# Own leading columns for each key slot, another split of the first tile's chunk sums, and new instruction orders in a one-core attention and gated-MLP kernel

## The chip, the cores and the metric

The kernel runs on one core of a Trainium2 chip. The core has five engines, each with its own instruction queue: TensorE (PE, with weight loads shown apart as PEld), VectorE (DVE), ScalarE (ACT), GpSimd (POOL) and SyncE (SP), which here only issues DMA transfers. ScalarE issues some transfers as well. Engines meet through semaphores. The metric is the device time of one execution in microseconds; smaller is better.

## The reference

The input x has 2048 tokens of 512 values. It is normalised, and the sum of two branches is added to it.

```
def _A_ref(x, wqkv, wo):                 # x is the normalised input
    H = 32; Dh = 16; W, dil = (8, 2)
    q, k, v = x @ wqkv                   # per head
    idx = pos[:, None] - off[None, :]    # each token sees itself and 7 tokens, 2 apart, behind it
    logits = einsum('bhsd,bhswd->bhsw', q, kg) * scale      # kg = k at idx; masked where idx < 0
    attn = softmax(logits)
    return einsum('bhsw,bhswd->bhsd', attn, vg) @ wo

def _B_ref(x, w_in, w_sp, b_sp, w_out):
    z = gelu(x @ w_in); z1 = z[..., :Fh]; z2 = layernorm(z[..., Fh:])     # Fh = 896
    g = einsum('ts,bsf->btf', w_sp, z2) + b_sp[None, :, None]             # 2048 x 2048 mix over tokens
    return (z1 * g) @ w_out

return x + _A_ref(xn, A_wqkv, A_wo) + _B_ref(xn, B_w_in, B_w_sp, B_b_sp, B_w_out)
```

## The kernel before

All on-chip data lie in one bf16 arena. Work is written as named tasks; a planner (`Plan`) works out dependences from the ranges that each task reads and writes, and puts in the semaphore waits. The order of the tasks on each engine is written out by hand in `plan.orders`: five lists, for TensorE, ScalarE, VectorE, GpSimd and SyncE's queue. An engine never passes a task that waits. The tasks that matter here are these, b being a block of 128 tokens, j a tile of four blocks (512 tokens), c one of four chunks of 128 of the 512 q and k columns, and t one of eight pairs of output blocks:

- `ldx b` loads a block of x; `bnst b`, `bnag b` (VectorE, L647, L650), `rstd b` (GpSimd, a power, L652) and `norm b` (VectorE, L662) normalise it; `xTd b` (SyncE, L666) transposes it by DMA. Blocks 0 to 3 are transposed on TensorE (`xTr`, `xTe`).
- `ldq` and `ldk` (L602) load the q and the k half of the attention weights.
- `Q j_c` and `K j_c` (TensorE, L730) are four matmuls each; `QKe j_c` (ScalarE, L738) evicts both from PSUM to a slot of q and of k, slot j mod 2.
- `prod j_c` (VectorE, L754) multiplies q by the eight shifted copies of k. It reads up to 14 columns ahead of the tile's own. For odd j these are the end of slot 0, which lies directly ahead of slot 1; for even j they are 16 leading columns (`KTpad`) ahead of slot 0, zero for tile 0 (`ktpad`) and copied by ScalarE from the end of slot 1 for tile 2 (`halo c`, L744).
- `padd j_n` (VectorE, L759) adds chunk products together; `lg j_0` (TensorE, L769) sums over the rows of a head with 8 matmuls for each array of products it is given, in tiles of 32 columns. In tile 0 chunks 0 to 2 are added on VectorE and the array of chunk 3 goes to TensorE by itself (`npadd` (1, 2)), so lg0_0 has 16 matmuls; in the other tiles all four are added first and there are 8. `lge j` (ScalarE, L791) evicts the logits.
- `z2_b`, `z1_b` (TensorE, L849, L892) and `V b` (L714) are the other projections, `z2g`, `z1g`, `Ve` their evictions on ScalarE, `z2s` (L904) squares for the variance. `zm, zq, ze, zv, zb j` are small VectorE steps of the second normalisation, `zr j` (L923) its power on GpSimd, `zn b` applies it (L930 on ScalarE for tiles 0 and 1, L934 on VectorE for 2 and 3). `T1` to `T4 j` (L951) are differences and sums of halves of z2.
- `pT`, `sm`, `ssub`, `sexp`, `sz`, `srec`, `sattn` are the softmax, by transposed tiles of logits.
- For each pair t: `w t` loads and transposes rows of w_sp (L959), `S13, S2, S4 t` (VectorE) add them, seven products `P1` to `P7` (TensorE, L1012) mix the tokens, `cA, cE, cB, g11, g21` (ScalarE) and `g12, g22` (VectorE) finish the gate, `u b` multiplies by z1 and `uT b` transposes the result; `pv b`, `pva`, `pvc t` (VectorE, L1142 to L1150) weigh the values and `OTd t` (L1154) transposes the attention output; `out b` (TensorE, L1204 and L1208) forms 512 output columns from `OTd` and `uT`, on top of x (`os`), and `fin` evicts them; `st` stores.
- `hm0` to `hm2` (GpSimd) make the head selector of lg, `mask0`, `mask1` the mask tile `maskt` that `smask` adds to tile 0; `ldb` loads b_sp into `bsb` and `biasf` (ScalarE) converts it. `Vhaloa`, `Vhalob`, `Vzero` shift v by a token row for pv.

Of PSUM's eight banks lg holds 6 and 7 and the projections share 0 to 5 in pairs, so a group waits for the eviction of the group three ahead of it.

Of the kernel before, what the change touches and what calls it, by code (L numbers as in the profile page):

```python
# [325 lines left out]
def build_kernel(nc, A_x, A_wqkv, A_wo, B_x, B_w_in, B_w_sp, B_b_sp, B_w_out, out, report=False, sched_kw=None,  # L326
# [88 lines left out]
    with ExitStack() as es:  # L415
# [808 lines left out]
        for t in range(NT):  # L1224
# [11 lines left out]
            if t >= 1:  # L1236
# [23 lines left out]
                z1g7 z1g5 zn5 z1g4 z1g2 z2s15 zn0 z1g0 z1g3 z1g1 lge3 Ve12 zn1 Ve13 zn2 Ve15 Ve14 zn3 Ve10 Ve7 Ve11  # L1260
                Ve6 ldxr1 Ve8 Ve9 ldxr0 Ve4 sexp3 Ve5 Ve2 Ve0 cA_0 Ve1 cE_0 Ve3 cB_0 sexp2 biasf g11_0 cA_1 g21_0 cE_1
                os12_0 cB_1 g11_1 os14_0 sexp1 g21_1 cA_2 cE_2 os15_0 cB_2 g11_2 cA_3 cB_3 g21_2 ldxr2 g11_3 fin14_0
                fin15_0 os13_0 cE_3 cA_4 st0_0_0 cB_4 g21_3 g11_4 fin12_0 os10_0 ldxr3 cE_4 fin13_0 os11_0 st1_0_0
                ldxr4 sexp0 cA_5 g21_4 os8_0 fin11_0 os6_0 cB_5 fin10_0 g11_5 cE_5 cE_6 cA_6 os9_0 g11_6 fin8_0
# [85 lines left out]
```

## Time and profile before

| | |
|---|---|
| time, median of 3 runs | 229.22 us (229.14 to 229.64) |
| profiled execution, its own time | 228.72 us |
| its span | 227.0 us |
| TensorE busy | 221.1 us (97%), 1170 matmuls recorded |
| VectorE busy | 209.8 us (92%), 258 instructions |
| ScalarE busy | 130.8 us (58%), 229 instructions |
| GpSimd busy | 36.9 us (16%) |
| granted TensorE clock | 1.00 |
| L754, prod | x16, 2283 ns each |
| L759, padd | x11, 2287 ns each |
| L769, lg | x40 matmuls of 32 columns, 383 ns each |
| L744, halo | x4, 203 ns each |
| L652, rstd on GpSimd | x16, 1180 ns mean |

The durations are of one profiled execution, whose span leaves out 1.7 us of its own time. Matmuls overlap: a matmul of 512 columns shows 379 ns, and two in a row start 216 ns apart (190 ns for 448 columns). Instructions of VectorE overlap by some 80 ns and those of ScalarE by some 100 ns where the next waits for nothing. The chain is the work that ended last, followed backwards.

### The profile page before, as it was taken

To read this page: it belongs to the slowest core of one execution; us is meant where nothing else is said; L and a number is where in the kernel's file an instruction comes from. 1 tells how busy PE (TensorE), PEld (TensorE's weight loads), DVE (VectorE), ACT (ScalarE), POOL (GpSimd) and SP (SyncE) were. 2 spreads that over 40 slices of the span, in tenths; PEclk is the share of its full clock that TensorE was granted. 3 is DMA by queue.
4 is the path that set the end of the run, shared out by engine and by line. 5 is a ranking of instruction groups with operands and counts; after the bars stand their busy time and mean duration, and the time that the engine had idled before them with its cause. 6 is when DMAs were issued, how large, how long until landed. Compare 5 with 4: busy or idle time off the path is not lost.

```text
span 227.0 us, 3128 instructions
## 1 busy us (share of the span) xinstructions
PE 221.1 (97%) x1170; PEld 121.9 (54%) x1184; DVE 209.8 (92%) x258; ACT 130.8 (58%) x229; POOL 36.9 (16%) x35
## 2 busy tenths in 40 slices
PE   8979999999999999999999999999999999999995
PEld 7535545454576776665555554445444544454444
DVE  4989999999999998999999999999999999999910
ACT  4757899689899999996253400614433234060732
POOL 4439929000441504000000000000000000000000
PEclk9999999999999999999999999999999999999999
DMA  6885435480000000989998999958958672629252
GB/s 221 257 235 137 90 60 118 79 244 0 3 0 0 0 0 18 250 177 215 248 176 130 209 177 148 210 127 168 178 124 175 129 173 97 123 90 171 105 122 92
DMA packets 77400, 29.96 MB, mean 132 GB/s; under 512 B 68669, under 2 KB 75339, under 8 KB 77259
## 3 DMA queue, kind: packets, MB, share of 16 engines
q1 hardware_dynamic: 74250, 25.08, 54.0%
q10 hardware_dynamic: 3136, 4.69, 6.4%
q8 instruction: 9, 0.15, 0.3%
q14 instruction: 5, 0.04, 0.1%
HBM read 9.05 MB, written 2.10 MB: 49 GB/s over the span
## 4 chain that ended last, share of the span: by engine, by line
PE 85%; DVE 5%; DMA 3%; POOL 3%; ACT 2%; issue 1%; SPq 0%; DVEq 0%
PE ps L1012 37%; PE ps L892 11%; PE ps L1208 11%; PE ps L730 9%; PE ps L714 6%; PE ps L1204 6%; PE ps L849 5%; POOL fpool L652 3%; DMA arena<-in_A_wqkv_dram 2%; DVE fpool L647 1%; DVE arena L759 1%; DVE arena L754 1%; DMA arena<-in_A_x_dram 1%; ACT arena L855 1%; ACT arena L904 1%
## 5 line engine op out<-in xcount | busy, mean ns | idle before, releaser
L1012 PE MATMUL ps<-arena 128*128 128x448 f16 (+1 forms) x448 | 86.6, 352 | 0.0
L1012 PEld LDWEIGHTS ps<-arena 128*128 128x128 f16 (+1 forms) x448 | 43.8, 98 | 41.4
L754 DVE TENSOR_TENSOR arena<-arena 128x4096 bf16<-128x4096 bf16 x16 | 36.4, 2283 | 0.5 <-ACT arena L738 0.4
L1142 DVE TENSOR_TENSOR arena<-arena 128x4096 bf16<-128x4096 bf16 x16 | 35.9, 2282 | 0.0
L1027 ACT ACTIVATE ps<-ps 128x448 f32<-128x448 f32 x16 | 8.5, 530 | 40.2 <-PE ps L1012 20.7
L730 PE MATMUL ps<-arena 128*128 128x512 bf16 x124 | 28.1, 379 | 1.4 <-DMA arena<-in_A_wqkv_dram 1.2
L1146 DVE TENSOR_TENSOR arena<-arena 128x4096 bf16<-128x4096 bf16 (+1 forms) x16 | 27.9, 1744 | 0.0
L1208 PE MATMUL ps<-arena 128*128 128x512 bf16 (+2 forms) x125 | 27.1, 355 | 0.1
L759 DVE TENSOR_TENSOR arena<-arena 128x4096 bf16<-128x4096 bf16 x11 | 25.2, 2287 | 0.1
L892 PE MATMUL ps<-arena 128*128 128x448 bf16 x128 | 24.8, 353 | 0.0
L730 PEld LDWEIGHTS ps<-arena 128*128 128x128 bf16 x128 | 14.3, 113 | 14.6 <-ACT arena L879 1.6
L892 PEld LDWEIGHTS ps<-arena 128*128 128x128 bf16 x128 | 18.4, 145 | 6.2 <-issue 0.4
L652 POOL TENSOR_TENSOR fpool<-fpool 128x1 f32<-128x1 f32 x16 | 18.8, 1180 | 13.4 <-DVE fpool L650 13.2
L1217 ACT ACTIVATE arena<-ps 128x512 bf16<-128x512 f32 (+2 forms) x17 | 9.4, 562 | 18.7 <-PE ps L1208 18.7
L738 ACT ACTIVATE arena<-ps 128x1024 bf16<-128x1024 f32 x16 | 16.0, 1023 | 7.3 <-PE ps L730 4.7
L849 PE MATMUL ps<-arena 128*128 128x448 bf16 x96 | 19.5, 353 | 0.6 <-ACT arena L738 0.6
L1208 PEld LDWEIGHTS ps<-arena 128*128 128x128 bf16 x126 | 11.9, 98 | 12.4
L923 POOL TENSOR_TENSOR fpool<-fpool 128x4 f32<-128x4 f32 x4 | 11.7, 2924 | 38.4 <-DVE fpool L921 32.0
L1030 ACT ACTIVATE arena<-ps,fpool 128x448 bf16<-128x448 f32 x16 | 10.0, 633 | 12.8 <-PE ps L1012 11.7
L1204 PE MATMUL ps<-arena 128*128 128x512 bf16 (+2 forms) x65 | 15.4, 353 | 0.4
L898 ACT ACTIVATE arena<-ps 128x896 bf16<-128x896 f32 x16 | 14.5, 913 | 1.2 <-PE ps L892 1.0
L904 ACT ACTIVATE arena<-arena 128x896 bf16<-128x896 bf16 x16 | 15.1, 946 | 0.1
(85 smaller groups left out, 242.8 us busy)
## 6 DMA issues: line engine op xcount, KB each, us to landing
arena<-in_A_x_dram ACTq DMA_DIRECT2D x8, 256.0 KB, 3.2
arena<-in_A_x_dram SPq DMA_DIRECT2D x15, 128.0 KB, 2.3
out_dram<-arena ACTq DMA_DIRECT2D x7, 256.0 KB, 2.1
arena<-arena SPq DMA_DIRECT2D x1, 1568.0 KB, 8.8
arena<-in_A_wqkv_dram SPq DMA_DIRECT2D x3, 512.0 KB, 4.5
arena<-in_B_w_in_dram SPq DMA_DIRECT2D x1, 896.0 KB, 5.2
arena<-in_B_w_out_dram SPq DMA_DIRECT2D x1, 896.0 KB, 5.3
arena<-arena SPq DMA_TRANSPOSE x40, 3.2
```

What stands on the lines that cost most here:

```text
L652: T("pool", lambda g: g.tensor_tensor(Fv("rstd", 1, b), Fv("mv", 1, 2 * b + 1), Fv("mhalf", 1), ALU.pow), reads=[("mv", b), "mhalf"], writ ...
L730: last = t.matmul(bank(k + which), AC(off["wqk"] + 1024 * dc + col0, [[4, 128]]), AC(off["xnT"] + dc * S + 512 * j, [[1, 512]]), start=(dc ...
L754: T("dve", lambda v: v.tensor_tensor(pbv, qb, kb, ALU.mult), reads=[("QT", c, j), ("KT", c, j), ("KT", c, j - 1) if j % 2 else ("KTpad", c ...
L759: T("dve", lambda v: v.tensor_tensor(A("pb", 4096, 4096 * a), A("pb", 4096, 4096 * a), A("pb", 4096, 4096 * b), ALU.add), reads=[("pb", b) ...
L849: last = t.matmul(ps[:, 512 * (k + hf): 512 * (k + hf) + HF], AC(off["xnT"] + dc * S + 128 * b, [[1, 128]]), AC(off["w_in2"] + FH * dc + H ...
L892: lastm = t.matmul(ps[:, 512 * (k + hf): 512 * (k + hf) + HF], AC(off["xnT"] + dc * S + b, [[NTOK, 128]]), AC(off["w_in1"] + FH * dc + HF ...
L904: T("act", lambda a: a.activation(A("sqj", FH), A("z2", FH, FH * b), ACTF.Square, accum_out=Fv("s2", 1, b)), reads=[("z2h", b, 0), ("z2h", ...
L1012: last = t_.matmul(pb_(k_), st(k), mv(k), start=(start and k == 0), stop=(k == 7), skip_group_check=True)
L1142: T("dve", (lambda iv, tv, av: lambda v: v.tensor_tensor(tv, iv, av, ALU.mult))(iv, tv, av), reads=[("attn", q // 4)] + [("V", i_) for i_ ...
L1146: T("dve", (lambda n: lambda v: v.tensor_tensor(AC(off["Vs"], [[4096, 2], [1, n]]), AC(off["Vs"], [[4096, 2], [1, n]]), AC(off["Vs"] + n, ...
L1204: t_.matmul(po, AC(off["OT"] + 1024 * (t % 3) + 512 * r_ + 128 * cc, [[1, 128]]), AC(off["wo"] + 512 * cc + c0, [[1, n]]), start=False, st ...
L1208: last = t_.matmul(po, AC(off["z1"] + FH * tb + 128 * fc, [[1, 128]]), AC(off["w_out"] + 512 * fc + c0, [[1, n]]), start=False, stop=(fc = ...
```

## The change

Each of the two key slots gets 16 leading columns of its own, so a row of keys is 16 + 512 + 16 + 512 columns long instead of 16 + 512 + 512. After each eviction of tiles 0, 1 and 2 ScalarE copies the last 16 columns of the keys into the leading columns of the next tile's slot (`halo j_c`, twelve copies instead of four), and prod reads its own slot alone. Tile 0 adds all four chunks on VectorE (`padd0_2` is new) and lg0_0 has 8 matmuls. maskt and bsb move into the place that holds v's last block later, so `Ve15` now comes after smask and biasf. All five orders are new; the list below shows them where they matter: the first part of each, and the ends of VectorE's and SyncE's. In SyncE's, the q half stands ahead of x9, x10, x11 and x8 and directly behind x4 to x7, the k half behind x9 and x10. Lines of the lists that are left out keep the same tasks in another order.

```diff
-    npadd=((1, 2), (1, 2, 3), (1, 2, 3), (1, 2, 3)),
+    npadd=((1, 2, 3), (1, 2, 3), (1, 2, 3), (1, 2, 3)),
-    KW = KP + 512 * NQ
+    KW = (KP + 512) * NQ
     off = {}
     base = 0
     off["W0"] = base
     off["V"] = base
     off["w_in2"] = base
     off["wqk"] = base + 4 * FH
+    off["maskt"] = off["wqk"] + 4096
+    off["bsb"] = off["maskt"] + 32
     base += 8192
     off["Vs"] = base
     off["QT"] = base
     base += 512
     off["Za"] = base
     base += 512
-    for name, n in (("R", 128), ("ident", 128), ("mx", 128), ("Zb", 256), ("hm", 32), ("maskt", 32), ("bsb", 16)):
+    for name, n in (("R", 128), ("ident", 128), ("mx", 128), ("Zb", 256), ("hm", 32)):
         off[name] = base
         base += n
         base = (base + 15) & ~15
             return off["QT"] + 2048 * (j % 2) + 512 * c
 
         def k_off(c, j):
-            return off["KT"] + c * KW + KP + 512 * (j % 2)
+            return off["KT"] + c * KW + KP + (KP + 512) * (j % 2)
 
         for c in range(4):
-            R(("KTpad", c), "sb", [(k_off(c, 0) - KP, k_off(c, 0))])
             for j in range(NJ):
+                R(("KTpad", c, j), "sb", [(k_off(c, j) - KP, k_off(c, j))])
                 R(("QT", c, j), "sb", [(q_off(c, j), q_off(c, j) + 512)])
                 R(("KT", c, j), "sb", [(k_off(c, j), k_off(c, j) + 512)])
         for s_ in range(NPB):
         R1("Za", "Za", 512)
         R1("sqj", "sqj", FH)
         R1("maskt", "maskt", 32)
+        R1("bsb", "bsb", 16)
         R1("zeros", "zeros", 512)
         for k in range(8):
             R(("ps", k), "ps", [(512 * k, 512 * k + 512)])
                                             fill=-1.0, base=0, channel_multiplier=1),
           writes=["nident"], est=350, name="nident1")
         T("pool", lambda g: g.memset(AC(off["KT"], [[KW, 4], [1, KP]]), 0.0),
-          writes=[("KTpad", c) for c in range(4)], est=200, name="ktpad", prio=2)
+          writes=[("KTpad", c, 0) for c in range(4)], est=200, name="ktpad", prio=2)
         def setup_masks():
             T("pool", lambda g: g.memset(hm, 1.0), writes=["hm"], est=150, name="hm0", prio=2)
             T("pool", lambda g: g.affine_select(out=hm, in_=hm, pattern=[[-4, 32]], compare_op=ALU.is_ge, fill=0.0,
                                             ACTF.Copy, scale=0.5),
               reads=[("ps", k), ("ps", k + 1)], writes=[("QT", c, j), ("KT", c, j)], est=c_act(1024),
               name="QKe%d_%d" % (j, c))
-            if j == 1:
-                T("act", lambda a: a.activation(AC(k_off(c, 2) - KP, [[1, KP]]), AC(ko + 512 - KP, [[1, KP]]), ACTF.Copy),
-                  reads=[("KT", c, 1)], writes=[("KTpad", c)], est=c_act(KP), name="halo%d" % c)
+            if j < NJ - 1:
+                T("act", lambda a: a.activation(AC(k_off(c, j + 1) - KP, [[1, KP]]), AC(ko + 512 - KP, [[1, KP]]), ACTF.Copy),
+                  reads=[("KT", c, j)], writes=[("KTpad", c, j + 1)], est=205, name="halo%d_%d" % (j, c))
 
         def prod_reduce(j):
             NPD = cfg["npadd"][j]
                 kb = AC(k_off(c, j), [[-2, 8], [1, 512]])
                 pbv = AC(off["pb"] + 4096 * s_, [[512, 8], [1, 512]])
                 T("dve", lambda v: v.tensor_tensor(pbv, qb, kb, ALU.mult),
-                  reads=[("QT", c, j), ("KT", c, j), ("KT", c, j - 1) if j % 2 else ("KTpad", c)], writes=[("pb", s_)],
+                  reads=[("QT", c, j), ("KT", c, j), ("KTpad", c, j)], writes=[("pb", s_)],
                   est=c_dve(4096, 2.0), name="prod%d_%d" % (j, c), prio=FILL)
 
             def psum(a, b, n):
# TensorE
 warm xTr0b fill0 xTr0a z2_0_0b z2_0_1b z2_0_0a xTr1a xTr1b z2_0_1a xNr z2_1_0a z2_1_0b z2_1_1a xTr2a
-xTr2b z2_1_1b z2_2_0a z2_2_0b xTr3a xTr3b z2_2_1a z2_2_1b z2_3_1a z2_3_1b z2_3_0a z2_3_0b K0_1 Q0_1
-K0_0 Q0_0 K0_2 Q0_2 K0_3 Q0_3 Q1_0 K1_1 K1_0 Q1_1 Q1_2 K1_2 K1_3 Q1_3 z2_4 z2_5 z2_6 lg0_0 z2_7 K2_1
-Q2_1 K2_0 Q2_0 Q2_2 z2_8 K2_2 K2_3 z2_11 Q2_3 z2_9 Q3_2 K3_2 Q3_0 K3_0 z2_10 lg1_0 K3_3 K3_1 Q3_1 Q3_3
-z2_13 z2_12 z2_14 z1_14 z2_15 z1_15 z1_13 z1_12 lg2_0 z1_10 z1_11 z1_8 z1_6 z1_9 z1_7 z1_5 z1_4 z1_2
-z1_0 z1_3 z1_1 lg3_0 V12 V13 V15 V14 V6 V10 V7 V11 V8 V9 V4 V1 V0 V5 V2 V3 P1_0 P5_0 P6_0 P2_0 P7_0
...
+xTr2b z2_1_1b z2_2_0a z2_2_0b xTr3b xTr3a z2_2_1a z2_2_1b z2_3_0a z2_3_1a z2_3_1b z2_3_0b Q0_0 K0_0
+Q0_1 Q0_2 K0_1 Q0_3 K0_2 K0_3 Q1_0 K1_0 K1_1 Q1_2 Q1_1 K1_2 Q1_3 K1_3 z2_4 z2_5 z2_6 z2_7 K2_0 Q2_0
+Q2_1 Q2_2 K2_1 K2_2 Q2_3 lg0_0 K2_3 z2_8 z2_9 z2_10 z2_11 K3_0 Q3_0 K3_1 K3_2 Q3_2 K3_3 Q3_3 Q3_1
+z2_13 lg1_0 z2_14 z2_12 z1_14 z1_15 z2_15 z1_13 z1_10 z1_12 z1_8 z1_11 lg2_0 z1_7 z1_9 z1_6 z1_2 z1_4
+z1_5 z1_1 z1_3 z1_0 V10 V11 lg3_0 V14 V12 V15 V13 V8 V4 V6 V9 V5 V7 V2 V3 V0 V1 P1_0 P5_0 P6_0 P2_0
+bits P3_0 P7_0 P1_1 P5_1 P4_0 P6_1 P2_1 P7_1 P3_1 P1_2 P4_1 P2_2 P6_2 P5_2 P7_2 P3_2 out14_0 P4_2 P1_3
...
# ScalarE
 actprime ldw_in2a_1 ldw_in2b_1 ldx2 ctr0 xTe0b xTe0a xTe1a xTe1b xNe z2g0_0 xTe2a xTe2b z2g0_1 z2g1_0
-xTe3a xTe3b z2g2_0 z2g1_1 z2g3_0 z2g2_1 QKe0_1 z2g3_1 QKe0_0 QKe0_2 QKe0_3 z2s0 QKe1_0 QKe1_1 z2s1
-QKe1_2 z2s2 QKe1_3 z2g4 z2s3 halo1 halo0 z2s4 z2g6 z2g5 z2s5 halo3 z2g7 QKe2_1 halo2 z2s6 QKe2_0 lge0
-z2g8 z2s7 QKe2_2 z2g11 z2s8 z2g9 QKe2_3 QKe3_2 QKe3_0 z2g10 z2s9 z2s10 QKe3_1 QKe3_3 z2s11 z2g13 z2g12
-zn6 z2g14 z1g14 z2s12 z2g15 z1g15 lge1 z1g13 z1g12 z2s13 zn7 z1g10 z1g11 z2s14 z1g8 z1g6 zn4 z1g9 lge2
...
+xTe3a xTe3b z2g2_0 z2g2_1 z2g1_1 z2g3_0 z2g3_1 QKe0_0 z2s0 QKe0_1 QKe0_2 QKe0_3 z2s1 QKe1_0 z2s2
+halo0_0 QKe1_1 QKe1_2 z2s3 QKe1_3 halo0_2 z2g4 halo0_3 halo1_0 z2g5 z2s4 z2g6 z2g7 z2s5 QKe2_0 z2s6
+halo0_1 z2s7 QKe2_1 QKe2_2 QKe2_3 halo1_2 lge0 z2g8 z2g9 z2s8 z2g10 z2g11 halo1_3 QKe3_0 halo2_2
+halo2_0 z2s9 QKe3_2 halo1_1 z2s10 QKe3_3 zn3 QKe3_1 halo2_1 z2g13 lge1 z2g14 z2g12 z2s11 z1g14 z1g15
+z2s12 z2g15 z1g13 zn2 z2s13 z1g12 z1g10 z1g8 z2s14 z1g11 z2s15 biasf z1g7 z1g9 zn4 z1g6 halo2_3 z1g2
+lge2 z1g4 z1g5 zn1 z1g1 zn6 z1g3 z1g0 Ve10 zn0 lge3 Ve14 zn5 Ve12 Ve15 ldxr0 Ve11 Ve13 zn7 Ve8 Ve4 Ve9
+Ve6 Ve5 ldxr1 Ve7 sexp3 Ve2 cA_0 Ve3 Ve1 cB_0 Ve0 g11_0 cE_0 cA_1 sexp2 os14_0 cE_1 cB_1 g21_0 g11_1
+cA_2 os15_0 g21_1 cB_2 cE_2 os12_0 g11_2 sexp1 cA_3 g11_3 fin14_0 g21_2 cB_3 os13_0 ldxr2 cE_3 ldxr3
+cA_4 sexp0 cB_4 fin12_0 g21_3 os11_0 fin15_0 cE_4 g11_4 os10_0 fin13_0 st0_0_0 cA_5 fin10_0 g11_5
+st1_0_0 ldxr4 g21_4 cB_5 cE_5 os9_0 os8_0 cA_6 fin11_0 ldxr5 os6_0 st2_0_0 cB_6 g21_5 g11_6 cE_6
+fin8_0 os7_0 ldxr6 fin6_0 fin9_0 os4_0 cA_7 cE_7 fin7_0 st3_0_0 cB_7 st4_0_0 g21_6 g11_7 os5_0 os2_0
...
# VectorE
-zeros steps0 steps1 bnst0 bnag0 ctr1 bnst1 bnag1 norm0 norm1 bnst2 bnag2 bnst3 norm2 bnag3 bnst4 bnag4
-norm3 bnst6 norm4 bnag6 bnst5 bnst7 bnag5 norm6 bnst9 bnag7 bnst8 bnag9 norm7 norm5 bnag8 bnst10
-bnst11 bnst12 bnag10 bnag11 bnag12 prod0_1 prod0_0 norm9 padd0_0 norm11 prod0_2 norm8 padd0_1 norm10
-prod0_3 bnst15 bnst14 norm12 bnag15 bnst13 bnag14 prod1_1 bnag13 prod1_0 norm15 norm13 padd1_0 norm14
-prod1_2 padd1_1 ze1 prod1_3 padd1_2 zm1 prod2_0 zq1 prod2_1 zv1 padd2_0 prod2_2 zb1 zm2 zm0_0 padd2_1
-ze2 zq2 prod2_3 zv2 ze0 zm0 padd2_2 zm3 prod3_0 zq3 zq0 prod3_1 padd3_0 zv0 prod3_2 zn11 smask zb2
-padd3_1 S13_0 prod3_3 zn10 zb0 padd3_2 zn8 ze3 zn9 zv3 S2_0 T3_1 T3_2 zn15 T1_2 zn14 zn12 zn13 T1_1
...
+zeros steps0 steps1 bnst0 bnag0 ctr1 bnst1 bnag1 norm0 norm1 bnst2 bnag2 bnst3 norm2 bnag3 norm3 bnst7
+bnag7 bnst6 bnag6 norm7 bnst5 norm6 bnag5 bnst4 norm5 bnag4 bnst9 bnst10 bnag9 norm4 bnag10 zm0_0
+bnst11 prod0_0 zm0 bnst8 bnag11 zq0 prod0_1 norm10 norm11 bnag8 bnst15 padd0_0 norm9 norm8 bnst12
+prod0_2 bnag12 bnag15 bnst14 bnst13 padd0_1 bnag14 bnag13 prod0_3 norm12 padd0_2 norm15 norm13 norm14
+prod1_0 prod1_1 ze0 padd1_0 zm1 prod1_2 zv0 padd1_1 prod1_3 zq1 zb0 padd1_2 ze1 prod2_0 prod2_1 zm2
+padd2_0 zv1 prod2_2 padd2_1 zq2 prod2_3 padd2_2 zb1 zm3 prod3_0 prod3_1 ze3 zq3 padd3_0 smask ze2
+prod3_2 zv2 padd3_1 zv3 prod3_3 padd3_2 S13_0 zn15 zn8 zn12 zn9 T3_0 zn13 zn10 S2_0 zn14 S4_0 T3_3
+zn11 T1_0 T1_3 T3_2 T2_0 sm1_3 T3_1 sm2_3 T2_3 sm3_3 T1_1 ssub3 T2_1 T1_2 T4_0 T4_3 T2_2 sz1_3 T4_1
+sz2_3 T4_2 sz3_3 sm1_2 srec3 sm2_2 sattn3 sm3_2 pv15 pv14 S13_1 g22_0 S2_1 g12_0 ssub2 pva2048_0 sz1_2
...
+S13_6 pva2048_4 g22_5 S2_6 pva1024_4 g12_5 pvc4 srec0 pv5 u4 pv4 u7 pva2048_5 S13_7 pva1024_5 S4_6
+pvc5 u5 sattn0 S2_7 pv3 g12_6 pv2 g22_6 pva2048_6 S4_7 pva1024_6 u2 pvc6 u3 pv0 g12_7 pv1 g22_7 u0
+pva2048_7 pva1024_7 pvc7 u1 zb3 fin1_1 zb2
# GpSimd
-mhalf ident0 ident1 nident0 nident1 ktpad rstd0 rstd1 rstd2 rstd3 rstd4 hm0 rstd6 mask0 rstd5 rstd7
-rstd9 rstd12 rstd11 rstd8 hm1 hm2 rstd10 rstd15 rstd14 rstd13 mask1 zr1 zr2 zr0 zr3
+mhalf ident0 ident1 nident0 nident1 ktpad rstd0 rstd1 rstd2 rstd3 mask0 rstd7 rstd6 rstd5 hm0 rstd4
+hm1 hm2 rstd10 rstd11 rstd9 rstd8 mask1 rstd15 rstd12 rstd13 rstd14 zr0 zr1 zr2 zr3
# SyncE queue
-ldx0 ldx1 ldw_in2a_0 ldw_in2b_0 ldx3 ldx4 ldx5 ldx7 ldx6 ldx9 ldx8 ldk ldx10 ldq ldx11 ldx12 xTd4 xTd5
-xTd6 xTd7 ldx14 ldx13 ldwv xTd9 ldx15 xTd8 xTd11 xTd10 xTd12 w0_0 xTd15 xTd13 xTd14 ldw_in1 w0_1 pT3
...
+ldx0 ldx1 ldw_in2a_0 ldw_in2b_0 ldx3 ldx7 ldx6 ldx5 ldx4 ldq ldx9 ldx10 ldk ldx11 ldx8 xTd7 xTd6 xTd5
+xTd4 ldx15 ldw_in1 ldx12 ldx14 ldx13 xTd11 ldb xTd10 xTd9 xTd8 xTd12 xTd13 xTd15 xTd14 w0_1 w0_0 ldwv
+ldwout pT3 pT2 pT1 pT0 w1_0 w1_1 Vhaloa w2_0 w2_1 Vzero Vhalob ldwo3 ldwo0 ldwo1 ldwo2 uT14 OTd0 uT15
+w3_0 w3_1 w4_0 uT13 uT12 w4_1 OTd1 uT10 w5_0 w5_1 uT11 OTd2 uT8 uT9 w6_0 w6_1 uT6 OTd3 w7_0 OTd4 w7_1
...
+uT4 uT7 uT5 OTd5 uT2 uT3 OTd6 uT0 OTd7 uT1 st7_1_0 st7_1_192
```

More of the change, by code (lines that the diff above doesn't have):

```diff
@@ L1260, in build_kernel @@
[L1260 to L1264, printed above, removed]
@@ L1268, in build_kernel @@
+                st7_0_0 fin1_2 st7_1_384
             """.split(),
             """
[L1270 to L1273 removed]
@@ L1274, in build_kernel @@
-                prod1_2 padd1_1 ze1 prod1_3 padd1_2 zm1 prod2_0 zq1 prod2_1 zv1 padd2_0 prod2_2 zb1 zm2 zm0_0 padd2_1
-                ze2 zq2 prod2_3 zv2 ze0 zm0 padd2_2 zm3 prod3_0 zq3 zq0 prod3_1 padd3_0 zv0 prod3_2 zn11 smask zb2
-                padd3_1 S13_0 prod3_3 zn10 zb0 padd3_2 zn8 ze3 zn9 zv3 S2_0 T3_1 T3_2 zn15 T1_2 zn14 zn12 zn13 T1_1
-                T2_2 T3_3 T2_1 T3_0 T4_1 sm1_3 T1_3 sm2_3 T1_0 zb3 sm3_3 S4_0 ssub3 T2_0 T4_2 T2_3 sz1_3 sz2_3 T4_0
-                sz3_3 sm1_2 T4_3 sm2_2 srec3 sm3_2 sattn3 ssub2 pv14 pv15 sz1_2 g22_0 sz2_2 sz3_2 S13_1 g12_0 S2_1
@@ L1290, in build_kernel @@
+                hm1 hm2 rstd10 rstd11 rstd9 rstd8 mask1 rstd15 rstd12 rstd13 rstd14 zr0 zr1 zr2 zr3
             """.split(),
             """
-                ldx0 ldx1 ldw_in2a_0 ldw_in2b_0 ldx3 ldx4 ldx5 ldx7 ldx6 ldx9 ldx8 ldk ldx10 ldq ldx11 ldx12 xTd4 xTd5
-                xTd6 xTd7 ldx14 ldx13 ldwv xTd9 ldx15 xTd8 xTd11 xTd10 xTd12 w0_0 xTd15 xTd13 xTd14 ldw_in1 w0_1 pT3
-                ldwout pT1 pT2 Vzero ldb pT0 w1_0 w1_1 Vhaloa w2_0 w2_1 Vhalob uT14 uT15 w3_0 w3_1 OTd0 ldwo1 ldwo2
-                ldwo0 ldwo3 uT13 uT12 w4_1 w4_0 OTd1 w5_0 uT10 uT11 w5_1 OTd2 uT8 OTd3 w6_0 w6_1 uT9 w7_0 OTd4 uT6
```

23 lines of the change are left out of this document (8 added, 15 removed).

## The prediction

> **What bounds the kernel now.** I read the page's busy times first, then the waits of TensorE, then the chain.
>
> ```profile
> PE 221.1 (97%) x1170; PEld 121.9 (54%) x1184; DVE 209.8 (92%) x258; ACT 130.8 (58%) x229; POOL 36.9 (16%) x35
> ```
>
> ```profile
> PE ps L730 <- DMA arena<-in_A_wqkv_dram: 1.2, 1, 1.2
> PE ps L619 <- PEq L1335: 0.8, 1, 0.8
> PE ps L849 <- ACT arena L738: 0.6, 1, 0.6
> ```
>
> ```profile
> 9.08 5.61 DMA arena<-in_A_wqkv_dram
> 14.68 0.14 issue
> 14.82 10.09 PE ps L730 x46
> ...
> 42.30 2.21 DVE arena L754
> 44.51 0.02 issue
> 44.53 1.03 ACT arena L738
> 45.57 0.04 issue
> 45.61 1.69 PE ps L849 x8
> ```
>
> TensorE (PE) has two real waits: for the second half of the q/k weights until 14.82, and at 45.61 for an eviction (L738) that waited for a product (L754). From 45.61 the chain is TensorE to the end. But VectorE (DVE) runs beside it just as closely. The stretches 86.2 to 105.3 and 105.3 to 216.5 of the table by windows (busy PE, PEld, DVE, ACT, POOL):
>
> ```profile
> 86.20:105.30 19.10, 18.84 (x96) 11.81 (x97) 17.54 (x41) 16.93 (x26) 2.46 (x1) 1.00 0.67 159
> 105.30:216.50 111.20, 110.83 (x564) 55.61 (x570) 110.66 (x117) 38.67 (x71) 0.00 (x0) 1.00 0.80 160
> ```
>
> In the last 111 us both are full. VectorE ends with pvc7 and two gate products, from VectorE's timeline:
>
> ```profile
> 213.59 0.69 DVE L1150 TENSOR_TENSOR arena<-arena 128x1024 bf16<-128x1024 bf16 x1
> 214.20 0.68 DVE L1054 SCALAR_TENSOR_TENSOR arena<-ps,fpool 128x448 bf16<-128x448 f32 x1
> 214.98 0.62 DVE L1036 TENSOR_TENSOR arena<-arena 128x896 bf16<-128x896 bf16 x1
> 215.84 0.62 DVE L1036 TENSOR_TENSOR arena<-arena 128x896 bf16<-128x896 bf16 x1 [0.23 <-ACT arena L1030]
> ```
>
> pvc7 ends at 214.28, its transpose OTd7 lands at 217.09 (2.81 later), u0's at 218.29; out0_0 needs both and starts at 219.72. So VectorE has 1.4 to 2.6 us in hand at the end. The forecast needs two sums: when TensorE reaches out0_0 by itself, and when OTd7 lands. The later one sets the end.
>
> **Sum for TensorE.**
> 1. Weights. Before, the fourth of x4 to x7 landed at 8.97 and q at 14.68; between them came x9, x8, k, x10 and q, 1,408 KB in 5.71 us, 247 KB/us. Now q, x9, x10 and k come in that stretch, 1,280 KB, 5.2 us: k lands at about 14.15, and the second group of matmuls, now K0_0, starts at 14.3 in place of 14.82: -0.5. Bounds: the quicker half took 4.15 us from issue to landing and the slower 5.61; from k's new issue near 8.75 (0.48 us an issue) that is 12.9, no wait at all (-1.3), to 14.36 (-0.3). I take the rate, which is from these very bytes. x11 and x8, issued behind k, shared the end of q's transfer before too.
> 2. lg0. Sixteen matmuls of L769 took 0.98 us (32.40 to the next block's 33.38), eight took 0.55 (52.20 to 52.75): -0.43.
> 3. The wait at 45.61 cost 0.99 between two matmul starts that stand 0.22 apart elsewhere: -0.77. QKe2_2 wrote over keys that prod1_2 read; with own leading columns it needs prod0_2 and halo0_2, both over 8 us earlier. QKe3_c still waits for prod1_c, as before, which comes 4 us ahead of it.
> 4. At 87.5 the first V group started 0.28 late after lg3_0. V10 and V11 now stand ahead of lg3_0, 1.5 us behind the eviction that frees their banks: -0.28.
>
> Together -2.0: TensorE alone would start out0_0 at 217.7.
>
> The twelve halo copies in place of four cost ScalarE eight times 0.203 us (L744) if nothing overlaps, 1.6; in a row they start 0.11 apart (31.32, 31.43, 31.54), 0.9. Eleven fall before 57 us, where ScalarE idles 5.2 us ahead of L738 alone: nothing for TensorE. The new waits are harmless by place: halo1_c waits for prod0_c (11 us old or more), halo2_2 for prod1_2 (2.4 us old), behind them QKe3_2 and QKe3_3. If that cover were gone, z2_13 would start later by up to 1.6; it has 1.3 in hand.
>
> **Sum for VectorE, to the end of pvc7.** Now u0 stands ahead of pvc7, so I start from u0's end before, 215.61.
> 1. The added padd0_2: L759, 2.287 us; the next instruction starts 0.08 ahead of an end, so +2.20.
> 2. The first product starts when QKe0_0 ends: K0_0 14.3 + 0.86, 0.19 to ScalarE, 1.03: 16.4, before 16.94: -0.5. VectorE idles 0.7 before norm3 (rstd3 ends at 8.91, before it was covered by bnst4), so bnst8, bnst12 and three bnag fall behind the first product and zm0_0 ahead of it: 2 x 0.59 + 3 x 0.10 - 0.08 = +1.4.
> 3. zb2 and zb3, which nothing reads, go behind the last use: -0.16.
> 4. Idle time that goes. norm10 and norm13 waited for rstd10 and rstd13 (gap plus the lost 0.08: 0.59 and 0.27), because GpSimd's instructions last as long as the product beside them: hm1 took 2.22 and rstd10 2.87, against 0.55 for rstd2. Now hm1, hm2 and rstd10 run before the first product. zn15 waited 0.98 for zr3; zv3 now comes two products earlier. sz1_3 waited 0.61 for the exponential; two more T operations now stand between. T3_0, prod2_2, pvc7 and u0 waited 0.18 each. Sum -3.2.
> 5. New idle: norm11 stands behind rstd11, which is issued beside prod0_1 and ends 0.41 after it (as rstd11 did after 19.23): +0.3.
>
> 215.61 + 2.20 + 1.4 - 0.5 - 0.16 - 3.2 + 0.3 = 215.65. OTd7 lands 2.81 later, 218.45, later than TensorE's 217.7. So VectorE sets the end: out0_0 starts near 218.4 instead of 219.72, -1.3. Adding the rows down the new orders one by one, with every wait, I get 218.2; I take -1.4. What follows out0_0 is the same work.
>
> Where TensorE meets VectorE on the way (TensorE's arrival / the sum or S operation done): lg1_0 55.3/54.2, lg2_0 71.1/70.3, lg3_0 87.1/86.7, P5_1 110.6/110.8 (S13_1), P6_2 124.4/124.6 (S2_2). The last two are where the first 0.35 us of the surplus goes.
>
> **Moved transfers on SP's queue.** ldw_in1 (896 KB, landed in 5.24) now precedes x12 to x14: they land near 24.5, needed at 26. ldb adds 0.49 ahead of xTd10, whose block is needed at 40. ldwv lands near 53, needed at 85. ldwout waits for the last z1 at 85.6, ahead of pT3, which waits for lge3 until 89 anyway. Vzero adds 1.0 ahead of Vhalob, which lands near 123.5; pv12 comes at 126.8. Ve15 now waits for smask and biasf (77 and 73, Ve15 at 91). w2 to w7 keep 2.8 us or more before their S13.
>
> **A rule against the change.** The busy row puts VectorE at 92% and PEld at 54%, and the change takes 0.43 us from TensorE to give VectorE 2.20. The Trainium skill, Perfetto Trace Analysis, Identifying the Most-Contended Engine, says to judge VectorE by occupancy and TensorE not by matmul time but by weight loads, and to relieve the fullest engine first; by it VectorE is the bound and the step is the wrong way round. The last row of windows agrees on VectorE (110.66 of 111.20); the 3.2 us of idle time above speak against its result. Its result is the third rival.
>
> **Rivals.**
> - TensorE alone decides: VectorE recovers more than I count, or k lands near 13. Then -2.0 to -2.4: 226.8 to 227.2. For it: the quicker half's 4.15. Against: VectorE's sum is 0.7 later.
> - No change: k lands at 15.6 or later (each us there moves the first product, and with it all of VectorE, by one). For it: half the x blocks still travel with it. Against: it is issued 0.3 earlier than q was, behind fewer bytes. Then 229.2.
> - Slower: VectorE pays in full. The place is pvc7; the price +2.20 and the 1.4 - 0.5 at the front, with none of the 3.2 recovered but 0.7 (zr3's wait and zb2/zb3 partly), because each instruction of GpSimd behind a product costs the product's 2.3 us and the waits return at norm11, norm8 and norm14. Then pvc7 ends at 215.61 + 2.20 + 0.9 - 0.7 = 218.0, OTd7 lands at 220.8, +1.1: 230.3. It decides as soon as VectorE loses over 1.3 us more than I count. For it: rstd13 and rstd14 still run beside products. Against: with 2.2 us of instructions between each bnag and its norm, norm14 has 0.1 in hand and norm8 0.4.
> - The release does not help, because another wait holds QKe2_c: then TensorE loses 0.77 again, 218.5, the same end as VectorE's; inside the forecast.
>
> **How the numbers follow.** The profiled execution took 228.72 us, its span 227.0; the median of the runs is 229.22. -1.4 gives 227.3 for it and 227.8 beside the median. A measurement can tell about 0.2%, 0.46 us. Forecast (227.2 to 228.7, k's landing and 0.4 us of unforeseen waits): 0.68. TensorE alone: 0.10, faster as well. No change: 0.10. Slower: 0.12. So faster 0.78, same 0.10, slower 0.12. The range 226.8 to 229.1 takes in the first two and half of the third.
>
> **What would show it.** Right: one TensorE wait of about 0.9 at K0_0 and none before an L849 group; eight matmuls in the first L769 group; twelve L759 instructions; 12 x 0.2 us in the halo line; the first product at 16.4; VectorE without a gap over 0.3 us from there to pvc7; out0_0 following OTd7's landing. Wrong: waits of VectorE for GpSimd over 1 us in total, a product waiting for a halo copy, k landing after 15, or pvc7 ending after 216.5.

## The result, and the profile after

The changed kernel took 230.84 us (median of 8 runs, 229.84 to 231.79), the kernel before 229.18 beside it: a ratio of 1.0074 (95% interval 1.0047 to 1.0102). It is slower by 1.7 us; the prediction had 1.4 us faster. The profiled execution took 229.84 us, the lowest of the eight, with a span of 228.1.

The busy times on the page of the profile:

```profile
PE 221.1 (97%) x1163; PEld 121.5 (53%) x1176; DVE 211.7 (93%) x259; ACT 131.1 (57%) x237; POOL 30.7 (13%) x35
```

TensorE's waits, and then VectorE's (us in total, times, longest), where before TensorE had waited 1.2 for the weights and 0.6 for an eviction:

```profile
PE ps L1207 <- DMA arena<-arena: 1.5, 1, 1.5
PE ps L1015 <- DVE arena L980: 0.9, 1, 0.9
PE ps L622 <- PEq L1339: 0.8, 1, 0.8
PE ps L733 <- DMA arena<-in_A_wqkv_dram: 0.4, 1, 0.4
```

```profile
DVE arena L974 <- DMA arena<-in_B_w_sp_dram: 1.9, 1, 1.9
...
DVE arena L665 <- POOL fpool L655: 1.1, 2, 0.7
```

Most lines stand three or four lower in the new file: L974 is S13, L980 S4, L962 the transpose of w, L1207 the first matmuls of an output. At the front nearly all went as forecast: the wait for weights fell from 1.2 to 0.4, the wait for an eviction at 45.61 is gone, and the two waits of VectorE for GpSimd in the list stand at norm1 and norm3, ahead of the first product. New are a wait of VectorE at S13_7, the first operation on w's last part, and two of TensorE at the end. The chain shows what follows from what:

```profile
181.54 8.99 DMA arena<-in_B_w_sp_dram
190.53 0.03 issue
...
190.63 1.23 DVE arena L974
...
217.47 3.26 DMA arena<-arena
220.86 1.02 PE ps L1207 x4
```

The transpose w7_1 was issued at 181.54 and landed 8.99 us later; before, it was issued at 182.76 and landed at 186.94, 4.18 later. S13_7 waited 1.92 for it. All of VectorE behind it came later by that much, pvc7 ended at 217.44, and OTd7 landed 3.26 after its issue, where before it took 2.78. The table by windows has the rest of the engines at that place, 185 to 190 us, before and after (busy PE, PEld, DVE, ACT, POOL, clock, DMA share, GB/s):

```profile
185.00:190.00 5.00, 5.00 (x27) 2.48 (x26) 5.00 (x6) 2.59 (x5) 0.00 (x0) 1.00 0.68 166
```

```profile
185.00:190.00 5.00, 5.00 (x26) 2.35 (x24) 3.71 (x3) 2.14 (x5) 0.00 (x0) 1.00 1.16 159
```

The DMA engines were far busier (1.16 against 0.68; the share adds up the times of packets, so packets in flight together can take it above 1) and moved no more bytes (159 against 166 GB/s). The timeline names what else was under way: before, the store of the third tile pair (L1179, issued by ScalarE) came 4 us behind w7_1; after, a load (ldxr5, L1166) and that store (st2_0_0, L1182) stand on either side of it.

```profile
182.76 1.93 SPq L959 DMA_TRANSPOSE arena<-in_B_w_sp_dram  x1
184.73 1.30 SPq L1038 DMA_TRANSPOSE arena<-arena  x1
186.76 0.35 ACTq L1179 DMA_DIRECT2D out_dram<-arena  x1
```

```profile
181.27 0.35 ACTq L1166 DMA_DIRECT2D arena<-in_A_x_dram  x1
181.54 3.92 SPq L962 DMA_TRANSPOSE arena<-in_B_w_sp_dram  x1
182.35 0.35 ACTq L1182 DMA_DIRECT2D out_dram<-arena  x1
```

The store took 7.98 us to land instead of 2.07, and SyncE needed 3.92 us to issue w7_1 instead of 1.93.

The theory, called the collision theory below: the new ScalarE order put a load and a store of 256 KB each beside w7_1, which slow it, and the new VectorE order asks for w7_1 sooner (S13_7 now stands ahead of pva1024_5, S4_6 and pvc5). The rivals: w7_1 is late through SyncE's own order, since OTd4 is issued right ahead of it (the SyncE-order theory); or VectorE's added sum (2.2 us) is the loss and the wait only its symptom (the VectorE-bound theory).

### The profile page after: what moved, and what is told of

Read it like the earlier page. It is cut to its first block, busy times and chain, and to the rows that moved or that the text cites. A ratio compares the mean times of both kernels' runs of the same rounds, so it can differ in the third digit from the quotient of the medians.

```text
span 228.1 us, 3127 instructions
## 1 busy us (share of the span) xinstructions
PE 221.1 (97%) x1163; PEld 121.5 (53%) x1176; DVE 211.7 (93%) x259; ACT 131.1 (57%) x237; POOL 30.7 (13%) x35
## 3 DMA queue, kind: packets, MB, share of 16 engines
q1 hardware_dynamic: 74250, 25.08, 54.6%
q10 hardware_dynamic: 3136, 4.69, 6.8%
## 4 chain that ended last, share of the span: by engine, by line
PE 73%; DVE 13%; DMA 9%; issue 3%; ACT 1%; POOL 1%; SPq 0%; DVEq 0%
PE ps L1015 27%; PE ps L733 12%; PE ps L895 11%; PE ps L852 8%; PE ps L717 6%; PE ps L1211 5%; DMA arena<-in_B_w_sp_dram 4%; DVE arena L1149 3%; DVE arena L1145 3%; PE ps L1207 3%; DMA arena<-in_A_wqkv_dram 2%; DMA arena<-arena 1%; DMA arena<-in_A_x_dram 1%; DVE arena L974 1%; PE ps L772 1%
## 5 line engine op out<-in xcount | busy, mean ns | idle before, releaser
L757 DVE TENSOR_TENSOR arena<-arena 128x4096 bf16<-128x4096 bf16 x16 | 36.4, 2287 | 0.2
L1145 DVE TENSOR_TENSOR arena<-arena 128x4096 bf16<-128x4096 bf16 x16 | 36.1, 2278 | 0.0
L762 DVE TENSOR_TENSOR arena<-arena 128x4096 bf16<-128x4096 bf16 x12 | 27.4, 2287 | 0.1
L895 PE MATMUL ps<-arena 128*128 128x448 bf16 x128 | 24.8, 353 | 0.0
L852 PE MATMUL ps<-arena 128*128 128x448 bf16 x96 | 19.0, 353 | 0.0
L655 POOL TENSOR_TENSOR fpool<-fpool 128x1 f32<-128x1 f32 x16 | 15.0, 945 | 17.3 <-DVE fpool L653 13.3
L1207 PE MATMUL ps<-arena 128*128 128x512 bf16 (+2 forms) x66 | 15.5, 353 | 1.9 <-DMA arena<-arena 1.5
```

What stands on the lines that cost most here:

```text
L757: T("dve", lambda v: v.tensor_tensor(pbv, qb, kb, ALU.mult), reads=[("QT", c, j), ("KT", c, j), ("KTpad", c, j)], writes=[("pb", s_)], est ...
L762: T("dve", lambda v: v.tensor_tensor(A("pb", 4096, 4096 * a), A("pb", 4096, 4096 * a), A("pb", 4096, 4096 * b), ALU.add), reads=[("pb", b) ...
L852: last = t.matmul(ps[:, 512 * (k + hf): 512 * (k + hf) + HF], AC(off["xnT"] + dc * S + 128 * b, [[1, 128]]), AC(off["w_in2"] + FH * dc + H ...
L895: lastm = t.matmul(ps[:, 512 * (k + hf): 512 * (k + hf) + HF], AC(off["xnT"] + dc * S + b, [[NTOK, 128]]), AC(off["w_in1"] + FH * dc + HF ...
L1145: T("dve", (lambda iv, tv, av: lambda v: v.tensor_tensor(tv, iv, av, ALU.mult))(iv, tv, av), reads=[("attn", q // 4)] + [("V", i_) for i_ ...
L1207: t_.matmul(po, AC(off["OT"] + 1024 * (t % 3) + 512 * r_ + 128 * cc, [[1, 128]]), AC(off["wo"] + 512 * cc + c0, [[1, n]]), start=False, st ...
```

## The experiments

Each ratio is to the kernel before, run beside it. The durations are those of each kernel's profiled execution.

**The changed kernel once more**, no edit.

> The changed kernel once more, for a second profile and its spread. The collision theory (the load ldxr5 and the store st2_0_0, issued by ScalarE, share the DMA engines with the transpose w7_1, which then takes 9.0 us in place of 4.2): w7_1 takes 7 to 10 us again, S13_7 waits 1.5 to 2.5 us, time 1.003 to 1.010 of the kernel before. If the long w7_1 of the first profile was a chance of that execution, it takes 4 to 5 us here and the time, near 229.8 to 231, must come from somewhere else. VectorE-bound theory (the added sum of 2.2 us alone): no wait at S13_7, pvc7 still ends after 217.

231.26 us, ratio 1.0092 (1.0064 to 1.0120). Its profile has a span of 230.2, 2.1 us over the first one's, and the chain shows half of it:

```profile
182.47 10.06 DMA arena<-in_B_w_sp_dram
192.62 1.23 DVE arena L974
...
219.47 3.29 DMA arena<-arena
```

w7_1 took 10.06, S13_7 waited 2.98 (1.06 more), and the other half is the front: the first product began at 17.09 instead of 16.15, since the k weights came later (TensorE waited 0.9 instead of 0.4). So the median lies above the first profile because both vary: the collision comes back, in other sizes.

**The load and the store later (e1).**

```diff
- ... fin11_0 ldxr5 os6_0 st2_0_0 cB_6 g21_5 g11_6 cE_6 fin8_0 os7_0 ...
+ ... fin11_0 os6_0 cB_6 g21_5 g11_6 cE_6 fin8_0 ldxr5 st2_0_0 os7_0 ...
```

> The changed kernel with ldxr5 and st2_0_0 three to four instructions later in ScalarE's order, behind fin8_0, so that w7_1 travels alone. Collision theory: w7_1 takes 4 to 5 us and lands by 186.5, S13_7 does not wait, pvc7 ends near 215.5 and OTd7 lands near 218.5; the time is 1.5 to 1.9 us under the changed kernel's, 228.7 to 229.4 (0.998 to 1.001 of the kernel before). SyncE-order theory (w7_1 is late because it is issued behind OTd4): w7_1 still takes 8 to 9 us, S13_7 waits 1.9, time as the changed kernel's, 1.007. VectorE-bound theory: w7_1 may land early, but pvc7 still ends after 217 and the time stays at 1.005 to 1.008.

228.27 us, ratio 0.9975 (0.9955 to 0.9996): 2.6 to 3.0 us under the changed kernel, more than the 1.5 to 1.9 expected, and a little under the kernel before. From VectorE's timeline, S13_7 (L974) behind pva2048_5, with no wait:

```profile
186.65 2.27 DVE L1149 TENSOR_TENSOR arena<-arena 128x4096 bf16<-128x4096 bf16 x1
188.85 1.21 DVE L974 TENSOR_TENSOR arena<-arena 128x2048 f16<-128x2048 bf16 x1
```

w7_1 took 5.54, and pvc7 ended at 215.65. That the sum is the loss, and that SyncE's order alone is, both fall. SyncE's order does have a small part in the 9 us. With OTd4 issued right ahead of it and still under way, w7_1 took 1.4 us more than before, though no load or store was beside it, and its issue took nearly as long as in the changed kernel:

```profile
180.47 1.23 SPq L1157 DMA_TRANSPOSE arena<-arena  x1
181.75 3.54 SPq L962 DMA_TRANSPOSE arena<-in_B_w_sp_dram  x1
```

Those 1.4 us cost no time here.

**w7_1 ahead of OTd4 (e2)**, the other way to bring it in time.

```diff
- ... OTd3 w7_0 OTd4 w7_1 uT4 ...
+ ... OTd3 w7_0 w7_1 OTd4 uT4 ...
```

> The changed kernel with w7_1 one place earlier in SyncE's order, ahead of OTd4. Collision theory: w7_1 is issued when w7_0 is, near 178 to 180, ahead of ldxr5 (181.3) and st2_0_0 (182.4), but still shares some of its time with them; it lands near 184 to 187, S13_7 waits less than 0.3 us; OTd4 takes the slow-down instead, and P-groups do not need it before out groups 8 and 9; time 1.2 to 1.9 us under the changed kernel's. SyncE-order theory: the same gain, with e1 gaining nothing. VectorE-bound theory: no gain.

228.16 us, ratio 0.9964 (0.9946 to 0.9981). w7_1 was issued at 180.20 and still took 7.79, landing at 187.99, before S13_7's turn at 189.19. It is not its duration that matters, but whether it lands in time. (OTd4 took 7.22 here; TensorE's waits for such transposes come to 0.4 us in the whole kernel.)

**The same collision in the kernel before (e3).**

```diff
- ... cB_5 fin10_0 g11_5 cE_5 cE_6 cA_6 os9_0 g11_6 fin8_0 st2_0_0 g21_5 cB_6 os7_0 fin9_0 ldxr5 ...
+ ... cB_5 fin10_0 g11_5 cE_5 cE_6 cA_6 os9_0 ldxr5 st2_0_0 g11_6 fin8_0 g21_5 cB_6 os7_0 fin9_0 ...
```

> The kernel before with ldxr5 and st2_0_0 moved up in ScalarE's order to stand right behind os9_0, as far beside w7_1 as they go. Collision theory: w7_1 takes 6 to 9 us in place of 4.2 and lands near 189 to 191 in place of 186.9; S13_7 stands at 191.5 there, so the wait is 0 to 0.5 us and the time is 0.999 to 1.003 of the kernel before. SyncE-order and VectorE-bound theories: w7_1 stays at 4 to 4.5 us, time unchanged.

229.18 us, ratio 1.0003 (0.9986 to 1.0019). w7_1 took 6.87 instead of 4.18 and landed at 190.01; S13_7 stands at 191.86 there. The collision alone costs the old order nothing: it needs the lost slack too.

**S13_7 later in VectorE's order (h)**, with both transfers left where the change put them.

```diff
- ... u7 pva2048_5 S13_7 pva1024_5 S4_6 pvc5 u5 ...
+ ... u7 pva2048_5 pva1024_5 S4_6 pvc5 S13_7 u5 ...
```

> The changed kernel with no transfer moved, but S13_7 behind pvc5 in VectorE's order, 2.4 us of VectorE's work later, so that part of the slack it had before is given back. Collision theory with the lost slack as its second half: w7_1 still takes 9 to 10 us, S13_7 waits 0 to 0.8 us, pvc7 ends 1.3 to 2.0 us earlier than in the changed kernel; time 0.998 to 1.002 of the kernel before. VectorE-bound theory, and any theory in which w7_1's lateness is a symptom: the wait only moves to S13_7's new place and the time stays at 1.007.

228.36 us, ratio 0.9971 (0.9950 to 0.9992). w7_1 took 9.66, S13_7 waited 0.12, and pvc7 ended at 215.85. So either half, the transfer or the place, takes the loss away by itself.

**Store alone late (g1), load alone late (g2)**, each the changed kernel with one of the two behind fin8_0.

```diff
  g1
- ... fin11_0 ldxr5 os6_0 st2_0_0 cB_6 ... fin8_0 os7_0 ...
+ ... fin11_0 ldxr5 os6_0 cB_6 ... fin8_0 st2_0_0 os7_0 ...
  g2
- ... fin11_0 ldxr5 os6_0 st2_0_0 cB_6 ... fin8_0 os7_0 ...
+ ... fin11_0 os6_0 st2_0_0 cB_6 ... fin8_0 ldxr5 os7_0 ...
```

> The changed kernel with only the store st2_0_0 moved behind fin8_0; the load ldxr5 stays beside w7_1. Collision theory, split by bytes (256 KB each): w7_1 takes 6 to 8 us in place of 9.0 and 10.1 and lands 1 to 2.5 us earlier; S13_7 waits 0 to 0.8 us; time 1.0 to 1.9 us under the changed kernel's, 0.999 to 1.003 of the kernel before. If the store alone does the harm: w7_1 takes 4 to 5.5 us, as in e1, 0.9975. If the load alone does it: 9 to 10 us, 1.007 to 1.009.

> The changed kernel with only the load ldxr5 moved behind fin8_0; the store st2_0_0 stays beside w7_1. Split by bytes: w7_1 takes 6 to 8 us, 0.999 to 1.003. If the load alone does the harm: w7_1 takes 4 to 5.5 us, 0.9975. If the store alone does it: 9 to 10 us, 1.007 to 1.009.

In g1 w7_1 took 5.98 and S13_7 did not wait for it; the time was 228.21 us, ratio 0.9963 (0.9943 to 0.9982). From the timeline of g2:

```profile
182.08 3.23 SPq L962 DMA_TRANSPOSE arena<-in_B_w_sp_dram  x1
182.89 0.34 ACTq L1182 DMA_DIRECT2D out_dram<-arena  x1
...
190.23 1.23 DVE L974 TENSOR_TENSOR arena<-arena 128x2048 f16<-128x2048 bf16 x1 [0.98 <-DMA arena<-in_B_w_sp_dram]
```

There w7_1 took 8.06 and S13_7 waited 0.98; the time was 228.60 us, ratio 0.9981 (0.9958 to 1.0004). Against e1's 5.54 the store alone adds 2.5 us and both together 3.5 to 4.5. The load alone adds 0.4, which is no more than chance: with neither beside it, w7_1 took 5.12 to 5.96 in four profiles (e1 and f1, f3, f4 below). A split by bytes does not fit: both move 256 KB.

The store differs from the load in its direction and in its issue, 0.8 us behind w7_1, where the load goes 0.3 ahead. The traces point to the issue. w5_0 is a transpose of the same kind, and of ScalarE's transfers no store is under way beside it, only the loads ldxr2 and ldxr3. In the profile of h it took 10.5 us, and the second load 9.2:

```profile
141.48 0.33 ACTq L1166 DMA_DIRECT2D arena<-in_A_x_dram  x1
...
141.85 3.48 SPq L962 DMA_TRANSPOSE arena<-in_B_w_sp_dram  x1
...
142.99 0.33 ACTq L1166 DMA_DIRECT2D arena<-in_A_x_dram  x1
```

Where ldxr3 was issued 1.1 to 1.4 us behind w5_0, w5_0 took 6.4 to 10.5 us (the changed kernel twice, e1, e2, h, f1, f3), and the load landed 0.2 us ahead of it each time. Where the two were issued within 0.15 us of each other, w5_0 took 6.1 to 6.5 (g1, g2, f4), and the load landed 1.9 us ahead. So a load can do what the store did, when it is issued behind the transpose; no run put the load into the store's place beside w7_1.

**The layout of before for the transposes' buffers (f1), and that of after in the kernel before (f2).** With its own leading columns for each slot the key buffer grew from 4160 to 4224 elements, so OT and all behind it moved by 128 bytes.

```diff
  f1 (from e1)
-    base = off["KT"] + 4 * KW
+    base = off["KT"] + 4 * KW + 64
     off["Za"] = base
+    off["mx"] = base + 384
...
  f2 (from the kernel before)
     base = off["KT"] + 4 * KW
+    off["hm"] = base
+    off["maskt"] = base + 32
+    base += 64
...
```

> e1 with 64 unused elements (128 bytes per partition) behind the keys, so that OT and all buffers behind it stand at the same offset against 256 bytes as in the kernel before; the scratch mx then lies in Za to make room. Layout theory: the wider key buffer (4224 in place of 4160 elements) moved the targets of the transposes OTd and uT by 128 bytes, and that is why OTd7 lands 3.24 to 3.29 us after its issue here and 2.79 to 2.81 in the kernel before. Then OTd7 takes 2.8, an undisturbed uT 2.6 to 2.7 in place of 2.9 to 3.0, and the time is 0.4 to 0.5 us under e1's: 0.995 to 0.997 of the kernel before. Rival (the transposes are slower because of what the new orders put beside them): OTd7 stays at 3.2 to 3.3, time as e1, 0.9975.

> The kernel before with OT and the buffers behind it moved up by the same 128 bytes (hm and maskt moved to stand between the keys and OT). Layout theory: OTd7 takes 3.2 to 3.3 us in place of 2.8, undisturbed uT 2.9 to 3.0; the end has 1.4 us in hand for them there, so the time is 0.999 to 1.003 of the kernel before. Rival: OTd7 stays at 2.8.

The eight transposes OTd, from issue to landing, in the kernel before, the changed one, f1 and f2, in this order:

```profile
DMA to landing us min/median/max: 2.8/3.4/6.0
```

```profile
DMA to landing us min/median/max: 3.2/3.3/5.0
```

```profile
DMA to landing us min/median/max: 2.8/3.3/5.4
```

```profile
DMA to landing us min/median/max: 3.2/3.7/6.0
```

The minima are those that travel alone, and they follow the address, not the order: OTd7 took 2.78 and 2.79 in the old layout with old orders (before, e3), 2.77 in f1, 3.21 to 3.29 wherever the buffer is moved, f2 with its old orders too. uT0 goes with it: 2.65 before, 3.04 in f2, 2.62 in f1. f1 took 228.00 us, ratio 0.9960 (0.9938 to 0.9982). That is 0.3 under e1, a difference that the intervals do not resolve; its first product began 0.83 later than e1's, so the profiles compare better from there to the first matmul of out0_0: 202.68 us in e1, 202.21 in f1. f2 took 229.03, ratio 0.9999 (0.9982 to 1.0017): before, VectorE had the slack for it.

**The weights' order alone, in the kernel before (b1).**

```diff
- ... ldx7 ldx6 ldx9 ldx8 ldk ldx10 ldq ldx11 ldx12 ...
+ ... ldx7 ldx6 ldk ldx9 ldx10 ldq ldx11 ldx8 ldx12 ...
```

> The kernel before with only the order of loads changed: k right behind the eighth x block, then x9, x10, q, x11, x8. The first groups there need both k and q in the order K0_1 Q0_1. Prediction's step 1 (TensorE waits for the second half of the weights; 0.5 us for the later x11 and x8): q lands 13.9 to 14.4 in place of 14.7, TensorE's wait shrinks from 1.2 to 0.4 to 0.8 us, and since TensorE sets the end of this kernel the time falls by 0.3 to 0.6 us, 0.997 to 0.999. Rival (the start is hidden behind later waits, at 45.61 above all): the wait at 45.61 grows by as much, time unchanged.

230.52 us, ratio 1.0065 (1.0042 to 1.0088): neither of the two came. q landed at 14.40, 0.28 sooner, but VectorE stood still:

```profile
15.16 0.70 DVE L647 BATCH_NORM_STATS2 fpool<-arena 128x6 f32<-128x512 bf16 x1 [1.67 <-DMA arena<-in_A_x_dram]
```

That is bnst8, waiting for x8, which the edit had put last; in the old VectorE order it stands ahead of the first product, which began at 18.57 instead of 16.94. So this order of loads, x8 last as in the change, pays only together with the new VectorE order, which has bnst8 behind that product.

**Without padd0_2 (f3), and with lg0_0 early as well (f4).**

```diff
  f3 (from e1), f4 (from f1)
-    npadd=((1, 2, 3), ...
+    npadd=((1, 2), ...
- ... norm12 padd0_2 norm15 ...
+ ... norm12 norm15 ...
  f4 too
- ... K2_0 Q2_0 Q2_1 Q2_2 K2_1 K2_2 Q2_3 lg0_0 K2_3 ...
+ ... K2_0 Q2_0 lg0_0 Q2_1 Q2_2 K2_1 K2_2 Q2_3 K2_3 ...
```

> e1 without padd0_2: the sum of the first tile is again left to TensorE (sixteen matmuls in lg0). VectorE then ends pvc7 2.2 us earlier at most, near 213.5 to 214, and OTd7 lands near 217; TensorE pays 0.43. Theory that VectorE's sum sets the end in e1 (the one on record): out0_0 starts when TensorE reaches it, near 218.0 to 218.4 in place of 219.0, time 0.6 to 1.0 us under e1's, 0.993 to 0.995 of the kernel before. Rival (TensorE sets the end in e1 as well, and OTd7's wait is only its shadow): 0.4 us over e1's, 0.999.

> f1 without padd0_2, and with lg0_0 (sixteen matmuls again) behind Q2_0 in TensorE's order, 4.6 us earlier than in f3, where prod1_0 had waited 4.3 us for it to free its buffer. Theory on record (after the collision and the layout, VectorE's sum and TensorE's stand within 0.5 us of each other at out0_0): VectorE runs 2.0 to 2.2 us earlier from prod1_0 on, TensorE pays 0.43 and now reaches out0_0 last; the wait for OTd7 is gone, and the time is within 0.3 us of f1's, 0.995 to 0.998 of the kernel before. Rival (VectorE is the bound all through, so that relieving it is what counts): 1.5 us or more under f1's, 0.990 or less.

f3 took 230.40 us, ratio 1.0059 (1.0037 to 1.0080). VectorE's waits tell why:

```profile
DVE arena L757 <- PE ps L772: 4.3, 1, 4.3
```

prod1_0 waited 4.26 for lg0_0 to read the second product buffer. The third sum does more than move 0.43 us from TensorE: it frees that buffer, and so lets lg0_0 stand late. f3 tested the order, not the sum. f4 mended it: 227.42 us (six runs, 227.04 to 227.69), 0.9926 (0.9899 to 0.9953), 1.6 us under the kernel before beside it and the fastest of all. But VectorE's 2.1 us of lead at prod1_0 (36.09 against 38.19 in e1) were spent again one tile on, at prod2_1, whose buffer lg1_0 frees:

```profile
56.34 2.29 DVE L758 TENSOR_TENSOR arena<-arena 128x4096 bf16<-128x4096 bf16 x1 [1.77 <-PE ps L773]
```

From the first product to out0_0 f4 took 202.00 us, f1 202.21. So the profile has the near balance that was expected (0.2 us) and no 1.5 us, and in f4 TensorE waits for nothing behind the weights. But the medians stand 0.6 apart, more than the 0.3 allowed, though the two intervals overlap. f4's runs spread over 0.65 us and f1's over 1.9. A late front in f1 does not explain the difference by itself: K0_0 began as much later there than in e1 (0.83) as the first product, and f4's TensorE would carry that to its end as well. So it stays open. Nor do the runs tell the missing sum from the earlier place of lg0_0: f4 has both, and no run has three sums with lg0_0 early.

## Why the prediction was wrong

**The front was right.** k landed at 13.96 (forecast 14.15), the first product began at 16.15 (16.4), the first L772 group has eight matmuls, there are twelve L762, and the twelve halo copies took 0.21 us each and kept nobody waiting. TensorE's wait for q and k fell by 0.8. That k came out so close is in part luck: the last of x4 to x7 landed at 9.85, not at 8.97, and the 1,280 KB behind it took 4.1 us instead of 5.2. One of the signs of being wrong came without harm: VectorE's waits for GpSimd add up to 1.1 us, over the 1 us named, but all of it ahead of the first product.

**VectorE's sum was right.** In e1, without the collision, pvc7 ended at 215.65; the sum had given 215.65. That it agrees to the last figure is luck: it had +0.3 at norm11, which was 0.12 in e1, so small errors cancel in it. The slower rival, VectorE paying in full through waits for GpSimd, did not come: the kernel is slower by another mechanism.

**TensorE's sum was 0.6 short, and this did not matter.** It had TensorE at out0_0 at 217.7. In e1 TensorE would have begun it at 218.3, 0.22 behind the start of the matmul before, if it had not waited for OTd7:

```profile
219.05 1.02 PE L1207 MATMUL ps<-arena 128*128 128x512 bf16 x4 [0.57 <-DMA arena<-arena]
```

Of the 0.6, 0.36 are the waits at P5_1 and P6_2, which the prediction named (0.35) and did not add. VectorE still came last, as forecast, but with OTd7 only 0.6 us behind.

**The step that failed** is the last sentence on moved transfers, "w2 to w7 keep 2.8 us or more before their S13". For w7_1 that holds only if it takes the 4.18 us of before, from 181.54 to 185.7, 3.0 us ahead of S13_7's turn at 188.71. It took 8.99 and 10.06: the duration belonged to the transfers beside it, and the change put others there. The paragraph looked at SP's queue alone, and the load and the store are in ScalarE's list. S13_7's wait for it was 1.9 us in the first profile and 3.0 in the second. A row of the trace of before spoke against a fixed duration, w5_0 beside OTd1 and ldxr2, which took 6.00 us and was hidden by slack:

```profile
141.78 1.26 SPq L1154 DMA_TRANSPOSE arena<-arena  x1
...
142.15 0.35 ACTq L1163 DMA_DIRECT2D arena<-in_A_x_dram  x1
...
143.08 3.44 SPq L959 DMA_TRANSPOSE arena<-in_B_w_sp_dram  x1
```

It was a warning and not yet the price: with 6.00 us w7_1 would have landed at 187.5, still 1.2 ahead of S13_7.

**A second term was mis-sized**: OTd7's landing, taken at 2.81 us behind pvc7's end, is 3.29. The diff showed the wider key buffer and the prediction did not ask what stands behind it: nearly 0.5 us, at the very end of the path. The two make up the miss at this point: the sum had OTd7 landing at 218.45, and it landed at 220.73 (217.47 + 3.26), 2.28 later; pvc7's end is 1.79 of it, the longer landing 0.48.

**A third point is the spread.** The prediction carried its profile's distance from the median (0.5 us) over to the new kernel; there the two medians lie 1.0 and 1.4 above the first profile. The second profile shows what varies: the collision and the first product's start, 1 us each.

With collision and layout both undone, f1's ratio, 0.9960, is 0.9 us faster than the kernel before: right in sign and two thirds of the 1.4 forecast.

**The rule against the change** was read in part. The Trainium skill (Perfetto Trace Analysis, Identifying the Most-Contended Engine) names MFU, the matmul work done as a share of the peak, beside the time of weight loads, and the prediction used the weight loads alone. TensorE's waits before came to 2.8 us of 227, so it was about as full as VectorE, and the 54% of weight loads does not make VectorE the only bound. f4, which leaves the sum with TensorE, is faster than f1, but by 0.2 us in the profile and 0.6 in the medians for 2.29 us of VectorE's work, and lg0_0's place changed with it; f3 shows the gain lost outright where the buffer that the sum frees is forgotten.
